# Moving part of a third row tile and one operand sum in a fused attention and MoE kernel

## The chip, the cores and the metric

The kernel runs on one core of one Trainium2 chip. The time is the device time of one execution in microseconds (us); the figure before is the median of three runs. One further execution was recorded by the hardware profiler, and every start and duration below is from that one.

The engines are named as in the profile: PE is the matmul engine (PEld its weight loads), DVE the vector engine, ACT the scalar engine, POOL the GpSimd engine, SP the queue that issues most DMAs. Each runs its own instructions in the order written. PSUM, where matmuls leave their results, has eight banks.

## What is computed

For 8 batches, 12 heads, 448 tokens and a head dimension of 64, attention with normalised q and k, followed by two matrix products with a leaky relu between them:

```python
q_n, k_n = rmsnorm(q, g_q), rmsnorm(k, g_k)
scores = (1 / sqrt(64)) * q_n @ k_n.T
attn = exp(scores - max(scores)); attn = attn / (sum(attn) + 1e-9)
x = (attn @ v) as rows of tokens            # 3584 x 768
h = x @ w_in                                # w_in: 768 x 2048
g = maximum(0.01 * h, h)
out = g @ w_out                             # w_out: 2048 x 768
```

Both w_in and w_out are the same for all tokens. Inputs and output are 32-bit floats; operands of the matmuls are rounded to 16 bits.

## The kernel before

**Attention.** The work is cut into 24 units `u`, each four heads of one batch, so three units make a batch. For a unit the kernel loads q and k (`load`), squares them (`prep_sq`), sums the squares (`prep_ssq`, line 186), forms the inverse root on ACT with a logarithm and an exponential (`prep_rinv`, 191 and 192), multiplies (`prep_norm`, 198) and transposes the result. Units up to 5 are transposed by PE matmuls (`prep_tr`, 210) that are copied out of PSUM by DVE, later ones by a DMA. The scores are computed for seven key tiles of 64 (`score`, 228), in four steps `d` = 0 to 3: key tile 0 in step 0 and the other six in steps 1 to 3. The exponential (`ex`, 243) subtracts a shift taken from key tile 0 alone. The shift's chain runs over three engines: DVE takes the maximum (257) and spreads it on a diagonal (259), PE multiplies this with a matrix of ones (276, or 282 in unit 3), and DVE reduces the product (277, 283) and forms the bias (287). The products with v (403), the sums of the exponentials (302, 313 or 340) and their inverse (387 to 394, or 361 and 366) give the attention output, which `xmul` (412) or line 381 multiplies into the tile `xt`, the operand of the first MoE product.

**First MoE product.** Per batch there are 16 row tiles `ft` of 128 of the hidden dimension, and each is a sum over six tiles `kt` of 128 of the model dimension, two from each unit of the batch. `moe1` (425) does one row tile in one bank, with six matmuls, then `prelu` (419) on ACT. For batch 0, row tiles 0 and 1 are done earlier, by `moe1_part` (433), in pieces between steps of units 2 and 3, into a pair of banks called `first`. Pieces 0 and 1 come from unit 0, 2 and 3 from unit 1, 4 and 5 from unit 2.

**Second MoE product.** Most token tiles are done in pairs by `seven`: seven block products in place of eight, with sums of operands. s1 to s4 (505 to 514) are DVE operations over blocks of `gt` and give the four blocks of the tile `sa`; the products `i0` to `i6` are PE items of eight matmuls each (535). i3 reads block 0 of sa, i4 block 2, i5 block 3 and i1 block 1. A call may be given the next pair of tiles, `nxt`, and then also issues s1 to s4 for that pair. The product banks are called ma, mb, mc and md; DVE adds (542) collect them into output tiles that SP stores.

**The order of the work** is written out by hand. `push` puts the items of one batch on a list, `queue`. `PLAN` has, for each unit from 3 on, a string of four digits, and the digit of step d is the number of items that `fill` takes from the list there. An item leaves its trailing DVE, ACT and store operations on a second list, `pend` (`later`), and the next item calls `flush`, which issues them before its own matmuls. At the end of step 3, flush can keep s1 to s4 back. In step 0 the order is: the scores of key tile 0, the maximum and the diagonal, flush, the products with v, the sums, the matmul with ones, the bias, the first exponential, then the items of the step.

In batches 1, 3 and 5 the first of two calls of `seven` has `nxt` and is not `mixed`. There i3 and i4 are the two items of step 3 of units 8, 14 and 20, and i5 and i6 the two items of step 0 of units 9, 15 and 21. In batch 7 the call is mixed, which means that parts of i0, i1 and i3 are issued in another order.

**The banks** are handed out from the list `free`. Up to unit 4, `aux` gives the longest free one of banks 0 to 3 and `slot` a pair out of banks 4 to 7; from unit 5 on all eight are shared. `drop` puts banks back at the end of the list.

Of the kernel before, what the change touches and what calls it, by code (L numbers as in the profile page):

```python
# [13 lines left out]
ts = bass.ts  # L14
# [4 lines left out]
def kernel(  # L19
# [11 lines left out]
    nc = tc.nc  # L31

    B, H, S, D = q.shape
    QH = 4
    NS = 7
    P = 128
# [3 lines left out]
    KT = DM // P  # L40
# [20 lines left out]
    def mine(i):  # L61
        return shared or i < 4
# [7 lines left out]
    def aux(bank=None):  # L70
        can = [i for i in free if mine(i) and bank in (None, i)]
        if shared:
            can = [i for i in can[:-1] if i ^ 1 not in free] or can
        free.remove(can[0])
        return single[can[0]]
# [12 lines left out]
    def drop(tile_):  # L88
        for i in range(8):
            if tile_ is single[i]:  # L90
                assert i not in free
                free.append(i)
                return
        x = [i for i in range(4) if tile_ is double[i]][0]
        assert 2 * x not in free and 2 * x + 1 not in free
        free.extend((2 * x, 2 * x + 1))
# [21 lines left out]
    win16 = cst.tile([P, NQ, 2, DF], FP16)  # L118
    wout16 = cst.tile([P, FT, DM], FP16)
    gt = cst.tile([P, FT, 8 * 64], FP16)  # L120
# [44 lines left out]
    def buf(u, name):  # L165
        if name not in st[u]:
            shape, dtype, bufs = SHAPES[name]
            st[u][name] = prep_p.tile(shape, dtype, tag=name[:2] if bufs == 3 and name != "qkT" else name, bufs=bufs, name=name)
        return st[u][name]
# [14 lines left out]
    def prep_ssq(u, c=ALL, tis=BOTH):  # L184
        for ti in tis:
            nc.vector.tensor_reduce(buf(u, "ssq")[:, ti, :, c[0]:c[1]], buf(u, f"sq{ti}")[:, :, c[0]:c[1]],  # L186
                                    axis=AXL.X, op=ALU.add)

    def prep_rinv(u, tis=BOTH):
        x = slice(tis[0], tis[-1] + 1)  # L190
        nc.scalar.activation(buf(u, "uu")[:, x], buf(u, "ssq")[:, x], AF.Ln, bias=eps_t, scale=1.0 / D)
        nc.scalar.activation(buf(u, "rinv")[:, x], buf(u, "uu")[:, x], AF.Exp, bias=0.0, scale=-0.5)  # L192
# [102 lines left out]
    xts = {}  # L295
# [119 lines left out]
    def prelu(b, dst, src):  # L415
        if b % 2 == 0:
            src = src.rearrange("p (t x) -> p t x", t=NS)[:, ::-1]
            dst = dst.rearrange("p (t x) -> p t x", t=NS)
        nc.scalar.activation(dst, src, AF.Prelu, bias=0.0, scale=1.0, alpha=0.01)  # L419
# [10 lines left out]
    def moe1_part(b, banks, k0, k1):  # L430
        for ft in range(2):
            for kt in range(k0, k1):
                nc.tensor.matmul(banks[:, ft, 0:S], win16[:, kt // 2, kt % 2, ts(ft, P)], xts[b][:, kt // 2, kt % 2],  # L433
                                 start=(kt == 0), stop=(kt == KT - 1))
# [4 lines left out]
    def store(pair, t, tile_, c, last):  # L439
        for y in range(2):  # L440
            n = 2 * t + (1 - y if t < 3 else y)
            b, grp = 2 * pair + n // NS, n % NS
            dst = out[b * S:(b + 1) * S, :].rearrange("(p t) m -> p t m", t=NS)
            eng = nc.scalar if last and y else nc.sync
            eng.dma_start(dst[:, grp, c], tile_[64 * y:64 * y + 64, c])
# [5 lines left out]
    def flush(keep=0):  # L451
        kept = [p for p in pend if keep and (p[0] in (s1, s2, s3, s4) or hasattr(p[0], "waits") or keep == 5 and hasattr(p[0], "copies"))]
        now = [p for p in pend if p not in kept]
        pend[:] = kept
        for fn, args in now:
            fn(*args)

    def out_tile():
        return opool.tile([P, DM], FP32, tag="ost", name="ost")
# [32 lines left out]
    def wblock(i, j):  # L492
        return wout16[:, HF * i:HF * i + HF, HC * j:HC * j + HC]
# [7 lines left out]
    def gblock(t, j):  # L501
        return gt[:, HF * j:HF * j + HF, ds(col(t), P)]
# [24 lines left out]
    def later(fn, *args):  # L527
        pend.append((fn, args))

    def seven(pair, tt, nxt=None, last=False, mixed=False):  # L530
        g = {}

        def mm(bank, a, b, first, fs=range(HF)):
            for f in fs:
                nc.tensor.matmul(bank[:, 0:HC], a[:, f], b[:, f], start=(first and f == 0), stop=(f == HF - 1), skip_group_check=not first)  # L535

        def bank(name):
            g[name] = aux()
            return g[name]

        def add(dst, src, name):
            nc.vector.tensor_tensor(dst, g[name][:, 0:HC], src, op=ALU.add)  # L542

        def put(i, c):
            store(pair, tt[i], g["o"][i], c, last)

        def i0():
            flush()
            g["o"] = (out_tile(), out_tile())
            ma = bank("ma")  # L550
            if mixed:
                mm(ma, gblock(tt[0], 0), wblock(0, 0), True, range(6))
                mm(bank("mb"), sa[:, 1], tw[:, 1], True, range(4))
            mm(ma, gblock(tt[0], 0), wblock(0, 0), True, range(6 if mixed else 0, HF))
            if mixed:
                mm(bank("mc"), sa[:, 0], tw[:, 0], True, range(4))
            later(lambda: nc.vector.tensor_copy(g["o"][1][:, L], g["ma"][:, 0:HC]))

        def i1():
            flush()  # L560
            mm(g["mb"] if mixed else bank("mb"), sa[:, 1], tw[:, 1], True, range(4 if mixed else 0, HF))
            later(lambda: add(g["o"][1][:, L], g["o"][1][:, L], "mb"))
            later(lambda: drop(g["mb"]))

        i1.merged = True

        def i2():
            flush()
            mm(g["ma"], gblock(tt[0], 1), wblock(1, 0), False)
            later(lambda: nc.scalar.copy(g["o"][0][:, L], g["ma"][:, 0:HC]))  # L570
            later(lambda: drop(g["ma"]))
            if last:
                later(put, 0, L)

        def i3():
            flush()
            mm(g["mc"] if mixed else bank("mc"), sa[:, 0], tw[:, 0], True, range(4 if mixed else 0, HF))
            later(lambda: add(g["o"][1][:, R], g["o"][1][:, L], "mc"))
            if nxt:
                later(s1, nxt)  # L580

        def i4():
            flush()
            mm(bank("md"), sa[:, 2], tw[:, 2], True)
            later(lambda: add(g["o"][1][:, R], g["o"][1][:, R], "md"))
            if last:
                later(put, 1, R)

        i4.merges = True

        def i5():
            flush()
            mm(g["mc"], sa[:, 3], wblock(1, 1), False)
            if nxt:
                later(s2, nxt)
            later(lambda: add(g["o"][0][:, R], g["o"][1][:, L], "mc"))
            later(lambda: drop(g["mc"]))
            later(put, 0, R if last else LR)
            if nxt:
                later(s3, nxt)  # L600
                later(s4, nxt)

        def i6():
            flush()
            mm(g["md"], gblock(tt[1], 1), tw[:, 3], False)
            def end():
                add(g["o"][1][:, L], g["o"][1][:, L], "md")
                drop(g["md"])
                put(1, L if last else LR)

            end.waits = True
            later(end)

        return [i0, i1, i2, i3, i4, i5, i6]

    HK = KT // 2
# [124 lines left out]
    queue = []  # L741
# [8 lines left out]
    def push(b):  # L750
# [32 lines left out]
        else:  # L783
# [8 lines left out]
            items += [(1.31, fn) for fn in std]  # L792
        queue.extend(items)

    PLAN = ("2122", "1222", "2112", "2122", "3232", "3322", "2322",
            "3222", "3232", "2222", "3323", "3232", "2322", "3222",
            "3232", "2222", "3323", "3232", "2322", "4356", "5232")
    STEPS = ((0,), (1, 2), (3, 4), (5, 6))
# [11 lines left out]
    def fill(u, d, jobs):  # L810
        for n in range(int(PLAN[u - 3][d])):
            fn = queue.pop(0)[1]
            fn()
            if jobs and not (d == 2 and (u == 12 and hasattr(fn, "merges") or u in (14, 20) and hasattr(fn, "merged"))):
                jobs.pop(0)()
        flush(keep=u if d == 3 and u < NU - 1 else 0)
        for job in jobs:
            job()
# [30 lines left out]
    with tc.manual_schedule():  # L849
# [56 lines left out]
        shift_mm(0)  # L906
        drop(st[0]["pb"])
        prep_ssq(1)

        def trn(u, ti, copy):  # L910
            prep_tr(u, ti, ((ALL, copy),))
# [32 lines left out]
        k1 = []  # L944
# [104 lines left out]
        ex(3)  # L1049
        prep_rinv(4)  # L1050
        moe1_part(0, first, KT - 2, KT - 1)
        moe1_part(0, first, KT - 1, KT)
        for ft in range(2):
            prelu(0, gt[:, ft, 0:S], first[:, ft, 0:S])
        drop(first)
        del queue[0:2]

        for u in range(3, NU):
            for d in range(4):
# [141 lines left out]
```

## Time and profile before

| | |
|---|---|
| median of three runs | 409.06 us (408.88 to 409.59) |
| profiled execution | 408.8 us |
| its span, first to last instruction | 406.9 us |
| PE busy | 396.7 us (97%), 3876 matmuls |
| DVE busy | 311.3 us (76%) |
| ACT busy | 303.9 us (75%) |
| POOL busy | 70.6 us (17%) |
| granted clock of PE | 1.000 |
| L505, s1 | 15 times, seven over 128x1024 and eight over 128x512 |

A row of the timeline gives start, duration, engine, line, instruction, output and inputs, shapes and the number of instructions merged into it. In square brackets stands how long the engine had been idle before it, and what released it. A matmul's duration reaches to the modelled end of its pipeline, so successive matmuls overlap in these rows, and the pitch from one start to the next is what they cost PE.

### The profile page before, as it was taken

Reading aid. Unit: us, or ns where it says so; the run is one execution under the profiler, and the core shown is the slowest. Engines: PE = TensorE matmul, PEld = TensorE weight load, DVE = VectorE, ACT = ScalarE, POOL = GpSimd, SP = SyncE. Lnnn points to the kernel's source line nnn. Section 1 sums busy time; section 2 is a strip of 40 time slices with the busy share of each in tenths; the row PEclk is TensorE's granted clock in tenths of the full one; section 3 lists DMA queues with packets and bytes.
Section 4 is the critical chain, followed back from the end, with each engine's and each line's share of the span. In section 5 each row is a group of like instructions: output and inputs, shape, how many; then the busy total and the mean of one; then the engine's idle time right before and its main releaser. Section 6 shows DMA issues by size and latency. Waiting matters only on the chain.

```text
span 406.9 us, 9527 instructions
## 1 busy us (share of the span) xinstructions
PE 396.7 (97%) x3876; PEld 225.0 (55%) x3876; DVE 311.3 (76%) x482; ACT 303.9 (75%) x474; POOL 70.6 (17%) x88
## 2 busy tenths in 40 slices
PE   8999999999999999999999999999999999999996
PEld 7665454555455544555455544555455557559963
DVE  5888999988879665886679756787679889567672
ACT  5998877788977699778978689868987667743600
POOL 1787432200120200120011200020002200000000
PEclk9999999999999999999999999999999999999999
DMA  6999999999455887478563795777732470022023
GB/s 197 276 235 251 240 235 246 236 223 213 96 156 110 239 216 117 135 198 192 137 159 66 226 218 116 187 178 170 177 72 49 122 169 0 20 68 79 0 57 99
DMA packets 72527, 62.87 MB, mean 154 GB/s; under 512 B 36389, under 2 KB 67621, under 8 KB 72485
## 3 DMA queue, kind: packets, MB, share of 16 engines
q1 hardware_dynamic: 61888, 50.08, 46.3%
q0 software_dynamic: 10272, 11.80, 18.8%
q8 instruction: 30, 0.49, 0.5%
q10 hardware_dynamic: 324, 0.39, 0.3%
q14 instruction: 13, 0.10, 0.1%
HBM read 45.61 MB, written 11.01 MB: 139 GB/s over the span
## 4 chain that ended last, share of the span: by engine, by line
PE 87%; DVE 2%; issue 0%; DVEq 0%
PE banks L425 29%; PE banks L535 25%; PE banks L228 9%; PE banks L471 8%; PE banks L669 6%; PE banks L403 6%; PE banks L340 3%; PE banks L276 1%; DVE banks L257 1%; DVE ost L542 1%; PE banks L210 0%; PE banks L433 0%; DVE xt L412 0%; DVE dg L259 0%; PE banks L313 0%
## 5 line engine op out<-in xcount | busy, mean ns | idle before, releaser
L243 ACT ACTIVATE et<-banks,eb 128x896 f16<-128x896 f32 x168 | 160.6, 1008 | 22.8 <-PE banks L228 22.1
L425 PE MATMUL banks<-xt,win 128*128 128x448 f16 x612 | 122.2, 353 | 0.0
L425 PEld LDWEIGHTS <-win 128*128 128x128 f16 x612 | 57.6, 98 | 56.2 <-issue 6.9
L419 ACT ACTIVATE gt<-banks 128x448 f16<-128x448 f32 x104 | 55.2, 551 | 9.1 <-PE banks L425 7.6
L186 DVE TENSOR_REDUCE ssq<-sq 128x14 f32<-128x896 f32 (+2 forms) x49 | 50.3, 1058 | 0.8 <-ACT sq L175 0.8
L228 PE MATMUL banks<-qkT 64*64 64x448 f16 x672 | 49.0, 361 | 1.6 <-DVE qkT L824 0.8
L535 PEld LDWEIGHTS <-sa 128*128 128x128 f16 x352 | 33.4, 98 | 26.1 <-issue 5.1
L535 PE MATMUL banks<-tw,sa 128*128 128x384 f16 x264 | 46.9, 326 | 0.0
L542 DVE TENSOR_TENSOR ost<-banks,ost 128x384 f32<-128x384 f32 x55 | 30.4, 553 | 13.2 <-PE banks L535 12.3
L257 DVE TENSOR_REDUCE banks<-banks 128x1 f32<-128x896 f32 x24 | 26.3, 1098 | 15.1 <-PE banks L228 11.1
L403 PE MATMUL banks<-et,vt 64*64 64x448 f16 x672 | 36.9, 349 | 0.0
L535 PEld LDWEIGHTS <-gt 128*128 128x128 f16 x264 | 25.5, 98 | 18.2 <-issue 1.7
L198 DVE TENSOR_TENSOR n<-rq,rinv 128x896 f16<-128x896 f32 (+2 forms) x25 | 33.1, 1328 | 1.9 <-ACT rinv L192 1.9
L471 PE MATMUL banks<-wout,gt 128*128 128x384 f16 x192 | 33.7, 326 | 0.0
L228 PEld LDWEIGHTS <-qkT 64*64 64x64 f16 x672 | 16.6, 105 | 29.1 <-issue 21.8
L535 PE MATMUL banks<-wout,gt 128*128 128x384 f16 x176 | 32.4, 326 | 0.0
L293 POOL COPY gate_t<-qkT 128x1 f16<-128x1 f16 x16 | 4.0, 251 | 152.3 <-DMA qkT<-n 152.3
L198 DVE TENSOR_TENSOR n<-rk,rinv 128x896 f16<-128x896 f32 (+2 forms) x26 | 26.1, 1012 | 0.0
L403 PEld LDWEIGHTS <-vt 64*64 64x64 f16 x672 | 20.0, 107 | 10.0
L471 PEld LDWEIGHTS <-gt 128*128 128x128 f16 x192 | 18.0, 98 | 13.7 <-issue 2.9
L325 DVE TENSOR_TENSOR ea<-et 128x896 f16<-128x896 f16 x14 | 10.0, 714 | 18.2 <-ACT et L243 18.2
L381 POOL TENSOR_TENSOR xt<-x,rz 128x896 f16<-128x896 f32 x8 | 16.6, 2077 | 32.3 <-DMA rz<-zs 26.0
(109 smaller groups left out, 492.4 us busy)
## 6 DMA issues: line engine op xcount, KB each, us to landing
rq<-in_q_dram SPq DMA_DIRECT2D x24, 448.0 KB, 5.2
rk<-in_k_dram SPq DMA_DIRECT2D x24, 448.0 KB, 6.0
out_dram<-ost SPq DMA_DIRECT2D x52, 192.0 KB, 3.0
rz<-zs SPq DMA_DIRECT2D x80, 112.0 KB, 3.6
vt<-in_v_dram POOLq DMA_DIRECT2D x24, 224.0 KB, 5.3
win<-in_moe_w_in_dram POOLq DMA_DIRECT2D x8, 384.0 KB, 14.7
wout<-in_moe_w_out_dram POOLq DMA_DIRECT2D x2, 1536.0 KB, 28.4
out_dram<-ost SPq DMA_DIRECT2D x4, 96.0 KB, 2.1
```

What stands on the lines that cost most here:

```text
L186: nc.vector.tensor_reduce(buf(u, "ssq")[:, ti, :, c[0]:c[1]], buf(u, f"sq{ti}")[:, :, c[0]:c[1]], axis=AXL.X, op=ALU.add)
L198: nc.vector.tensor_tensor(buf(u, "n16")[:, ti, c[0]:c[1]].rearrange("p s a d -> p a s d"), src[:, :, c[0]:c[1]], buf(u, "rinv")[:, ti, :, ...
L228: nc.tensor.matmul(banks[a][64 * r:64 * r + 64, 0:S].rearrange("p (t x) -> p t x", t=NS), kT(u, r, a, t), qT(u, r, a), start=True, stop=True)
L243: nc.scalar.activation(s["et"][:, t], sT[:, :, 0:S], AF.Exp, bias=s["eb"], scale=1.0)
L257: nc.vector.tensor_reduce(s["spare"][:, 511:512], sT[:, :, 0:S], axis=AXL.XY, op=ALU.max)
L403: nc.tensor.matmul(s["pv"][r][64 * a:64 * a + 64, 0:S], vts[u % NV][64 * r:64 * r + 64, a, t], s["et"][64 * r:64 * r + 64, t, a], start=(t ...
L419: nc.scalar.activation(dst, src, AF.Prelu, bias=0.0, scale=1.0, alpha=0.01)
L425: nc.tensor.matmul(hps[:, 0:S], win16[:, kt // 2, kt % 2, ts(ft, P)], xt[:, kt // 2, kt % 2], start=(kt == 0), stop=(kt == KT - 1))
L471: nc.tensor.matmul(op2[:, 0:HC], gt[:, ft, ds(col(t), P)], wout16[:, ft, ds(HC * half, HC)], start=(i == 0), stop=(i == FT - 1))
L535: nc.tensor.matmul(bank[:, 0:HC], a[:, f], b[:, f], start=(first and f == 0), stop=(f == HF - 1), skip_group_check=not first)
L542: nc.vector.tensor_tensor(dst, g[name][:, 0:HC], src, op=ALU.add)
L669: nc.tensor.matmul(bank[:, HX * i:HX * i + HX].rearrange("p (t x) -> p t x", t=NS), w, x[:, kt], start=start, stop=(kt == HK - 1), skip_gr ...
```

## The change

There are two edits.

The first one is at the place where batch 0's row tiles 0 and 1 are finished. A new function, `moe1_third`, issues `moe1`'s matmuls of row tile 2 for a range of kt. Its first four are put between kt 4 and kt 5 of the first two row tiles, its last two behind kt 5, and its prelu behind the two others. Row tile 2 is taken off the list, and the first digit of `PLAN` goes from 2 to 1, so that all later steps get the same items as before.

The second edit concerns `seven` where it is not mixed: s1 of the next pair is left on `pend` by i5, just ahead of s2, where i3 left it before.

```diff
@@ seven, i3
-            if nxt:
+            if nxt and mixed:
                 later(s1, nxt)
@@ seven, i5
             flush()
             mm(g["mc"], sa[:, 3], wblock(1, 1), False)
             if nxt:
+                if not mixed:
+                    later(s1, nxt)
                 later(s2, nxt)
             later(lambda: add(g["o"][0][:, R], g["o"][1][:, L], "mc"))
             later(lambda: drop(g["mc"]))
@@ PLAN
-    PLAN = ("2122", "1222", "2112", "2122", "3232", "3322", "2322",
+    PLAN = ("1122", "1222", "2112", "2122", "3232", "3322", "2322",
@@ new function
+        def moe1_third(bank, k0, k1):
+            for kt in range(k0, k1):
+                nc.tensor.matmul(bank[:, 0:S], win16[:, kt // 2, kt % 2, ts(2, P)], xts[0][:, kt // 2, kt % 2],
+                                 start=(kt == 0), stop=(kt == KT - 1))
@@ ahead of the loop over units
         moe1_part(0, first, KT - 2, KT - 1)
+        third = aux()
+        moe1_third(third, 0, KT - 2)
         moe1_part(0, first, KT - 1, KT)
+        moe1_third(third, KT - 2, KT)
         for ft in range(2):
             prelu(0, gt[:, ft, 0:S], first[:, ft, 0:S])
+        prelu(0, gt[:, 2, 0:S], third[:, 0:S])
         drop(first)
-        del queue[0:2]
+        drop(third)
+        del queue[0:3]
```

## The prediction

> **What bounds the kernel now.** I read the page first (busy shares, clock row, the chain that ended last), then the waits of the matmul engine (PE) alone, stretch by stretch, then the chain and the timeline around each wait. The page gives PE 97% busy, its clock full in all 40 slices, and the chain that ended last runs 87% through PE. So time is won only where PE stands idle. Its waits over the whole span, as "engine line waited for: us in total, times, longest us":
>
> ```profile
> PE banks L276 <- DVE dg L259: 1.2, 3, 0.4
> ...
> PE banks L433 <- DVE xt L412: 0.5, 1, 0.5
> ```
>
> The same view cut into stretches shows none from 48 us to the end but the three of L276, at 125.67, 219.03 and 312.56. PE is unbroken between them, and what one of them gives up moves the end, unless something else then makes PE wait. The other row is the single stall at 42.48. The change touches exactly these two rows.
>
> The first of the three, in order of time (start us, us, engine, line, instruction):
>
> ```profile
> 121.68 1.08 DVE L198 TENSOR_TENSOR n<-rk,rinv 128x896 f16<-128x896 f32 x1
> 122.68 0.54 DVE L542 TENSOR_TENSOR ost<-banks,ost 128x384 f32<-128x384 f32 x1
> ...
> 123.14 0.68 DVE L505 TENSOR_TENSOR sa<-gt 128x1024 f16<-128x1024 f16 x1
> ...
> 123.74 0.55 DVE L542 TENSOR_TENSOR ost<-banks,ost 128x384 f32<-128x384 f32 x1
> 124.21 1.08 DVE L257 TENSOR_REDUCE banks<-banks 128x1 f32<-128x896 f32 x1
> ...
> 125.18 0.10 PEld L276 LDWEIGHTS <-onesp 128*128 128x128 f16 x1 [0.18 <-issue]
> 125.33 0.29 DVE L259 TENSOR_TENSOR dg<-ident,banks 128x128 f16<-128x128 f16 x1
> 125.67 0.22 PE L276 MATMUL banks<-dg,onesp 128*128 128x128 f16 x1 [0.42 <-DVE dg L259]
> ```
>
> VectorE (DVE) is the late one: it comes from a 2.92 us normalisation at 118.83, then does the add of i3, s1 (L505), the add of i4, and only then the shift's maximum (L257) and diagonal (L259), while PE has its weights for L276 at 125.18. The scores that L257 reads ended near 123.33, long before its start.
>
> The stall at 42.48:
>
> ```profile
> 41.19 0.58 ACT L394 ACTIVATE rz<-rz 128x448 f32<-128x448 f32 x1
> ...
> 41.80 0.62 DVE L412 TENSOR_TENSOR xt<-banks,rz 128x448 f16<-128x448 f32 x1
> ...
> 42.34 1.08 DVE L186 TENSOR_REDUCE ssq<-sq 128x14 f32<-128x896 f32 x1
> 42.48 0.54 PE L433 MATMUL banks<-xt,win 128*128 128x448 f16 x2 [0.50 <-DVE xt L412]
> ...
> 45.07 1.09 DVE L198 TENSOR_TENSOR n<-rk,rinv 128x896 f16<-128x896 f32 x1
> 45.22 0.14 PEld L228 LDWEIGHTS <-qkT 64*64 64x64 f16 x8 [0.37 <-issue]
> ...
> 45.72 0.89 PEld L210 LDWEIGHTS <-n 128*128 128x128 f16 x14 [0.36 <-issue]
> ```
>
> What to see: behind the stall, PE's transposes of unit 4's k need the n that DVE ends at 45.07 + 1.09 = 46.16. That chain runs over L394, L412, L186, Ln and Exp at 43.46 and 43.81, and the norms at 44.06 and 45.07. No PE work of after 41 us is in it.
>
> **Part 1, the third row tile.** Nothing is added or removed in all: six matmuls, one prelu and one bank move from step (3,0) to before it. The 12 matmuls of L425 that follow the stall take 2.27 us, 0.19 each. After the change four of them fill 41.98 to 42.74; the last key tile of the first two, ready at 42.44, goes at 42.74, 0.26 later than now; two for the third follow to 43.5, and row tile 3 to 44.6. PE then reaches the scores of (3,1) at 45.22 - 0.50 = 44.72 and the transposes at 45.22. The first seven have their n since 45.15. The second seven are held by 46.16. They are held there today already: cut finely, the weight loads of the first seven are over by 46.12, none runs until 46.22, and there they resume, 0.06 after DVE's end. So the 0.50 is not saved but moves to 45.7, and PE's work from 46.22 on stands where it stood: **0.00**. Cover for the 0.26 and for the earlier prelu: ScalarE (ACT) starts its four prelus at 43.94 behind rinv, whatever PE does, and the third tile is complete near 43.5; without that cover 0.26 would be paid. The bank: the third takes bank 1, last read by an L392 that started at 40.63 and took 0.53; row tile 3 then takes bank 2 and the free list at (3,1) is the old one, so no later bank changes. The weights are those that row tile 2 reads today. No DMA moves with it. Bounds: -0.50, if the transposes were not held, and +0.26, if the cover failed; I take 0 because the hold is a row of the trace.
>
> **Part 2, s1 behind the chain.** In the three non-late odd batches, s1 leaves the flush of i4, at (8,3), (14,3), (20,3), for the flush of i6, behind the shift's chain of the next unit. Three instructions of 0.68 us move; none is added, no DMA, no wait.
>
> Before the chain: the add of i4 now starts at 123.74. It reads what the add of i3 writes, which ends at 122.68 + 0.54 = 123.22; dependent DVE instructions follow after some 0.03 (s1 at 116.34 for 0.42, s2 at 116.79). PE's i4 ended near 123.0. So it starts at 123.25, 0.49 earlier, and L257, L259 with it: dg ends at 125.13 and L276 could start at 125.18. PE's own side: its weights are loaded at 125.18, and an unhindered L276 starts 0.01 after its load (at 80.62 and 80.63), so 125.19. Both sides allow 125.67 - 125.19 = 0.48. The second place gives 219.03 - 218.56 = 0.47 (DVE: 217.10 - 216.62 = 0.48), the third 312.56 - 312.09 = 0.47 (DVE 0.49). **Sum 1.42.** The lower bound is the printed waits, 0.42 + 0.41 + 0.41 = 1.24; the upper is DVE's 0.60 from s1's start to the next start, three times 1.80, which PE's own readiness cuts off. I take 1.42, because it goes by starts.
>
> A rule speaks against it. The Trainium skill, VectorE: DVE Perf Modes, section "The DRAIN you can't avoid", says that after each DVE operation a flush of about its duration less 266 ns has to pass before the next one starts. By that an add of 0.54 would hold the next for another 0.27, the gain would be near 0.24 a place and 0.72 in all. Here 122.68 to 123.14 is 0.46 from start to start, less than the first one's duration, so I go by the rows.
>
> Behind the chain: s1 now stands between eb (L287) and s2. Today s2 starts at 126.40 and the adds follow. After, L277 is released either by L276 (125.5) or by ACT's copy at L355, which ends at 124.77 + 0.91 = 125.68 and is named as the releaser of L277 five times elsewhere. Take the later: L277 at 125.70, eb at 126.03, s1 126.10, s2 126.70, the add to mc 127.30, s3 127.77, s4 128.37, the add to md 128.97 to 129.52 (pitches 0.60 and 0.47, as now). So DVE runs at most 0.1 behind today while PE runs 0.48 ahead. Who waits for that: i0 of the next seven takes mc's bank at 129.18 - 0.48 = 128.70, free from 127.86, slack 0.84; i1 takes md's bank one item of 1.30 later, at 130.0, free from 129.52, slack 0.48; sa block 1 is needed at 130.0 and done at 127.4. The store (SP queue) waits for the mc add, 0.1 later at most. That the writes of s1 and s2 don't wait for i5's matmuls is seen today: s2 starts at 126.40 while they read sa until 127.19. DVE catches up in its 1.58 us of idling before 134.58. So I cost this side at nothing; with the 0.48 used up, every further tenth costs 0.1 a place.
>
> **Sum.** 0.00 - 1.42: the span goes from 406.9 to 405.5 and the profiled execution from 408.8 to 407.4, 1.9 us lying outside the span. That execution is 0.26 under the median of 409.06; the same step from the median gives 409.06 - 1.42 = 407.64, forecast **407.65**.
>
> **Rivals.**
> - *The transposes let go as well.* Part 1 keeps its 0.50: 409.06 - 1.42 - 0.50 = 407.15. For it: PE is idle at 42.0 by the profile. Against: the loads that resume at 46.22, 0.06 behind n. Chance 0.05.
> - *A half gain.* The add of i4, or L257, starts later than reckoned, or L276 finds another wait, so that a place gives half, 0.24: 409.06 - 0.72 = 408.35. For it: two sides of the sum meet within 0.01 us, so any delay on DVE's counts. Against: the start-to-start rows. 0.11.
> - *The stall is replaced.* PE wins 0.48 at L276 and waits as long for something else before the unit ends: 409.06. For it: DVE is 76% busy and carries s1 in any case. Against: the slack of 0.48 and no PE wait from 126 to 216 today. 0.08.
> - *Slower: md's bank.* The add to md in i6's tail, now queued behind s1 and s2, ends after i1 wants the bank. PE then waits, and it decides for a loss once that add is late by more than 0.48 of slack plus the 0.48 won, 0.96. One more pair of the reductions of L186 ahead of it on DVE (2.07 us for two, as at 47.46) would cost 2.07 - 0.96 = 1.11 a place: 409.06 + 3.33 = 412.4. For it: 0.48 is a thin slack, and a normalisation beside POOL's product took 2.92 instead of 1.08 at 118.83. Against: in the order written out, the only jobs between i5 and i6 are ACT's exponentials and loads. 0.06.
>
> The forecast keeps 0.70. **Range** 407.1 to 408.6: below, the first rival; above, the half gain with the median's own scatter (the three runs lie within 0.7). Apart from the rivals the forecast's own range is 407.3 to 408.0. What a measurement can tell from no change is 0.2%, 0.8 us. Faster by more: the forecast, the first rival and about a third of the half gain, 0.79; within it: the rest of the half gain and the replaced stall, 0.15; slower 0.06.
>
> **What would show it.** In the profile after: the row "L276 waits for dg" is gone or at 0.1 in all, L505 (128x1024) stands behind L287 at all three places, and L257 starts 0.5 after the scores' first matmul instead of 1.3. For part 1: no wait at L433, but a PE wait for n at L210 of about 0.5 near 46.2, and PE's row tile 4 starts where it starts now, near 46.6. Wrong would be: a PE wait at L535 or L425 between 126 and 132, a wait at L210 under 0.3, or L276 still waiting 0.2 or more.

## The result and the profile after

The changed kernel takes **407.66 us** (median of 7 runs, 407.21 to 408.14) against 409.06 (7 runs, 408.36 to 409.59): a ratio of 0.9965, 95% interval 0.9953 to 0.9976. That is 1.4 us, and between 1.0 and 1.9 by the interval. The profiled execution took 407.55, its span 405.7. Faster, by an amount that can be told from no change, and close to the forecast of 407.65. How close is partly luck, as the terms below show.

The waits of PE over the whole span, after (engine, line, waited for: us in total, times, longest us):

```profile
PE banks L840 <- DVE onesp L107: 1.2, 1, 1.2
PE banks L210 <- DVE n L198: 1.0, 2, 0.6
PE banks L228 <- DVE qkT L826: 0.8, 2, 0.4
PE banks L228 <- ACT et L243: 0.7, 4, 0.2
PE banks L885 <- DVE n L198: 0.4, 1, 0.4
PE banks L302 <- DVE qkT L826: 0.2, 1, 0.2
```

The rows of L276 and L433 are gone. L210 had one wait of 0.6 before, at 33.70 us; it now has a second one of 0.4. From 48 us to the end PE waits for nothing that the profile names.

The first of the three places, in order of time:

```profile
122.81 1.21 DVE L542 TENSOR_TENSOR ost<-banks,ost 128x384 f32<-128x384 f32 x2
...
123.94 1.09 DVE L257 TENSOR_REDUCE banks<-banks 128x1 f32<-128x896 f32 x1
...
125.06 0.29 DVE L259 TENSOR_TENSOR dg<-ident,banks 128x128 f16<-128x128 f16 x1
...
125.32 0.10 PEld L276 LDWEIGHTS <-onesp 128*128 128x128 f16 x1 [0.18 <-issue]
125.40 0.22 PE L276 MATMUL banks<-dg,onesp 128*128 128x128 f16 x1
...
125.72 0.30 DVE L277 TENSOR_REDUCE banks<-banks 128x1 f32<-128x128 f32 x1 [0.38 <-PE banks L276]
...
126.13 0.68 DVE L505 TENSOR_TENSOR sa<-gt 128x1024 f16<-128x1024 f16 x1
...
126.85 0.69 DVE L508 TENSOR_TENSOR sa<-sa,gt 128x1024 f16<-128x1024 f16 x1
...
129.13 0.55 DVE L542 TENSOR_TENSOR ost<-banks,ost 128x384 f32<-128x384 f32 x1
...
130.15 1.46 PE L535 MATMUL banks<-tw,sa 128*128 128x384 f16 x8
```

The two adds (x2) now run back to back and L257 follows at once; s1 (L505) stands behind the bias. PE's multiplication with ones starts 0.08 behind its weight load, where it was 0.49 before. The last two rows are md's release and i1, which takes that bank: 129.13 + 0.55 = 129.68 against 130.15.

Around the transposes, the place of the first edit (L914 is the third row tile):

```profile
41.97 0.92 PE L914 MATMUL banks<-xt,win 128*128 128x448 f16 x4
...
42.72 0.54 PE L433 MATMUL banks<-xt,win 128*128 128x448 f16 x2
...
45.22 1.08 DVE L198 TENSOR_TENSOR n<-rk,rinv 128x896 f16<-128x896 f32 x1
...
45.41 0.56 PE L210 MATMUL banks<-ident,n 128*128 128x128 f16 x7
...
46.36 0.56 PE L210 MATMUL banks<-ident,n 128*128 128x128 f16 x7 [0.39 <-DVE n L198]
...
46.76 1.30 PE L425 MATMUL banks<-xt,win 128*128 128x448 f16 x6
```

The stall at 42.5 is filled, and 4 us later the transposes of k stand still until DVE's n, 45.22 + 1.08 = 46.30. Row tile 4 starts at 46.76. Before, it started at 46.62, in a profile in which everything from 39.8 on lies 0.15 earlier.

To read such small shifts, all profiles are set at the start of `moe1_part`'s second group of matmuls (40.63 before). The table gives, in us and good to 0.01, how much earlier (-) or later (+) L276 starts than in the first profile of before, and how the last matmul's end moves. The columns are named by the start before. 55.84 lies behind the first edit; 125.67, 219.03 and 312.56 are the three places of the second.

| kernel | 55.84 | 125.67 | 219.03 | 235.07 | 312.56 | end |
|---|---|---|---|---|---|---|
| changed kernel | -0.01 | -0.42 | -0.84 | -1.01 | -1.42 | -1.43 |
| e1, second edit alone | -0.01 | -0.42 | -0.84 | -1.01 | -1.42 | -1.43 |
| e2, first edit alone | -0.01 | -0.02 | -0.04 | -0.21 | -0.22 | -0.22 |
| e3, row tile 4 between | -0.38 | -0.80 | -1.22 | -1.39 | -1.80 | -1.52 |
| e4, s1 twice ahead | -0.01 | +0.72 | +1.45 | +1.59 | +2.32 | +2.31 |
| e5, add behind | -0.01 | -0.51 | -0.98 | -1.14 | -1.63 | -1.63 |
| e6, s3 three times | -0.01 | -0.42 | +0.61 | +1.62 | +1.20 | +2.38 |
| e7, both moves | -0.37 | -0.88 | -1.35 | -1.51 | -2.00 | -2.00 |
| e8, e3 without the first edit | +0.05 | -0.39 | -0.79 | -0.97 | -1.37 | -1.07 |
| e9, before once more | -0.01 | -0.01 | -0.01 | -0.19 | -0.18 | -0.19 |
| e10, e3 with small settings | -0.37 | -0.79 | -1.20 | -1.37 | -1.76 | -1.77 |
| e11, e7 once more | -0.37 | -0.87 | -1.33 | -1.49 | -1.97 | -1.96 |
| e12, e5 once more | -0.01 | -0.49 | -0.96 | -1.12 | -1.60 | -1.59 |

### The profile page after: what moved, and what is told of

Its sections match the earlier page's. It is cut to its first block, busy times and chain, and to the rows that moved or that the text cites. A ratio compares the mean times of both kernels' runs of the same rounds, so it can differ in the third digit from the quotient of the medians.

```text
span 405.7 us, 9527 instructions
## 1 busy us (share of the span) xinstructions
PE 396.8 (98%) x3876; PEld 225.2 (56%) x3876; DVE 310.3 (76%) x482; ACT 303.6 (75%) x474; POOL 71.0 (17%) x88
## 4 chain that ended last, share of the span: by engine, by line
PE 88%; DVE 1%; issue 0%; ACT 0%
PE banks L425 29%; PE banks L535 25%; PE banks L228 9%; PE banks L471 8%; PE banks L403 7%; PE banks L671 6%; PE banks L340 3%; PE banks L276 1%; DVE n L198 1%; PE banks L210 0%; DVE ssq L186 0%; PE banks L433 0%; PE banks L313 0%; DVE xt L412 0%; DVE ost L542 0%
## 5 line engine op out<-in xcount | busy, mean ns | idle before, releaser
L535 PEld LDWEIGHTS <-sa 128*128 128x128 f16 x352 | 33.4, 98 | 24.9 <-issue 3.9
L535 PE MATMUL banks<-tw,sa 128*128 128x384 f16 x264 | 46.9, 326 | 0.0
L257 DVE TENSOR_REDUCE banks<-banks 128x1 f32<-128x896 f32 x24 | 26.3, 1098 | 15.4 <-PE banks L228 12.2
L535 PEld LDWEIGHTS <-gt 128*128 128x128 f16 x264 | 25.5, 98 | 18.0 <-issue 1.4
L198 DVE TENSOR_TENSOR n<-rq,rinv 128x896 f16<-128x896 f32 (+2 forms) x25 | 32.0, 1281 | 2.4 <-ACT rinv L192 2.4
L535 PE MATMUL banks<-wout,gt 128*128 128x384 f16 x176 | 32.4, 326 | 0.0
L570 ACT COPY ost<-banks 128x384 f32<-128x384 f32 x11 | 5.3, 478 | 22.7 <-PE banks L535 22.7
```

The source lines that it names most:

```text
L198: nc.vector.tensor_tensor(buf(u, "n16")[:, ti, c[0]:c[1]].rearrange("p s a d -> p a s d"), src[:, :, c[0]:c[1]], buf(u, "rinv")[:, ti, :, ...
L257: nc.vector.tensor_reduce(s["spare"][:, 511:512], sT[:, :, 0:S], axis=AXL.XY, op=ALU.max)
```

## The experiments

### The two edits apart (e1, e2)

e1 is the kernel before with only this:

```diff
-            if nxt:
+            if nxt and mixed:
                 later(s1, nxt)
...
             if nxt:
+                if not mixed:
+                    later(s1, nxt)
                 later(s2, nxt)
```

> Only the second edit: s1 behind the shift's chain, row tile 2 where it was before. Theory (the first edit is worth nothing, because the stall it fills comes back at the transposes of unit 4's k): the time of the changed kernel, 407.7, within 0.2%, and L276 at the three places 0.4 earlier each, relative to the place before. Rival (the first edit is worth its 0.5 of filled stall): 408.2, and PE's row tile 4 some 0.5 later than in the changed kernel.

e2 is the rest of the change: `moe1_third`, its calls, the shorter list and PLAN "1122".

> Only the first edit: part of the third row tile ahead of the last key tile, s1 where it was. Theory: no change, 409.1; no wait at L433, a wait of 0.4 at the transposes (L210) in its place, and L276 still waiting 0.4 at the three places. Rival (the stall is saved): 408.6, and every later start 0.5 earlier.

Measured: e1 407.76 (10 runs), ratio 0.9960 (0.9947 to 0.9973); e2 408.81 (11 runs), ratio 0.9990 (0.9980 to 1.0000), both beside 409.15. PE's waits from 39 us on, in e1:

```profile
PE banks L433 <- DVE xt L412: 0.5, 1, 0.5
```

and in e2:

```profile
PE banks L276 <- DVE dg L259: 1.2, 3, 0.4
PE banks L210 <- DVE n L198: 0.4, 1, 0.4
```

e1 keeps the stall at L433 and still stands, from 55.84 to the end, within 0.01 of the changed kernel. e2 exchanges one row for another and has won 0.01 at 55.84. So by the traces the second edit is the whole gain, and the first is worth nothing by itself, as forecast: its stall comes back at the transposes. Of the 0.22 that e2 shows at the end, 0.17 come from the stretch between 219 and 235, which is taken up at e9.

### Is PE held by n and by nothing else? (e3, e8)

e3 puts other work where PE now stands still. On top of the changed kernel:

```diff
-    PLAN = ("1122",
+    PLAN = ("1022",
...
                     for ti in range(2):
                         prep_tr(u + 1, ti, VV)
+                        if u == 3 and ti == 0:
+                            queue.pop(0)[1]()
```

> The changed kernel with one more move: in step (3,1) the item of that step, row tile 4 of the first product, goes between the transposes of unit 4's q and those of its k. Theory (PE is held there by DVE's n for k and by nothing else): the six matmuls, 1.14, cover the hold of 0.39; PE waits no more at L210 near 46.4 and all later starts are 0.35 to 0.4 earlier: 407.3. Rival (the hold was never worth time, since ACT's exponentials bound that stage): the wait is gone but the scores of (3,2) wait for ACT in its place, 407.7.

e8 does the same without the first edit (PLAN "2022", row tile 2 in its old place).

> The second edit alone (row tile 2 where it was before), with row tile 4 between the transposes of unit 4's q and k. Theory (without the first edit the transposes are hardly held, 0.06, so that there is little to cover, while the stall of 0.50 at 42.5 stays): 407.7, and 0.35 to 0.4 more than the same move on top of the changed kernel. Rival (the move alone brings the gain, the first edit has no part in it): the time of that one, 407.3.

Measured in e3, in order of time:

```profile
45.44 0.56 PE L210 MATMUL banks<-ident,n 128*128 128x128 f16 x7
...
45.84 1.30 PE L425 MATMUL banks<-xt,win 128*128 128x448 f16 x6
...
46.98 0.56 PE L210 MATMUL banks<-ident,n 128*128 128x128 f16 x7
```

Row tile 4 covers the hold, no wait is printed there, and the table has 0.38 at 55.84, which stays until 312.56. e8 has +0.05 there, so the same move costs a little where the transposes are not held. The move puts the copy of k (L826) behind row tile 4 and DVE's later work with it, so that L276 waits for the diagonal: in e8 its weights are there from 56.57, the diagonal ends at 56.40 + 0.29 = 56.69, and it starts at 56.74. By the traces the first edit is therefore worth 0.43 once something covers the hold, and nothing without it. ACT, the rival, did not take the place of the wait.

In the medians the gain of e3 did not show: 407.87 (8 runs), ratio 0.9966 (0.9952 to 0.9980), and e8 407.95 (11 runs), 0.9977 (0.9968 to 0.9985). Part of this is in the last column: both lose some 0.3 at the last unit's shift. In e3:

```profile
343.15 0.34 PE banks L228 x4
343.49 0.12 issue
343.61 0.06 DVE u L684
343.67 0.48 issue
344.15 1.10 DVE banks L257
```

(the chain that ended last: start, length, what it runs through). A DVE add, L684, starts at 343.61, though DVE had been idle for 0.26 and PE's matmuls for it were over at 343.15. It starts 0.90 after the add before it, where the changed kernel has 0.54. e10 looks at this.

### How PE's wait hangs on DVE's queue (e4)

On the kernel before, i3 leaves s1 twice:

```diff
             if nxt:
                 later(s1, nxt)
+                if not mixed:
+                    later(s1, nxt)
```

> The kernel before, with s1 issued twice in a row where it stood before the change (the second writes the same values again), in the three batches concerned: 0.60 more DVE work ahead of the shift's chain at three places. Theory (the length of DVE's queue ahead of the chain sets PE's wait at L276, one for one): L276 waits 1.0 in place of 0.4 at each, 409.06 + 1.8 = 410.9. Rival (the wait at L276 is set by something else, and s1 gave way to another delay): 409.1 to 409.5.

Measured: 411.06 (9 runs), ratio 1.0044 (1.0031 to 1.0056), 1.9 above the 409.15 beside it. PE's waits from 48 us on:

```profile
PE banks L276 <- DVE dg L259: 3.4, 3, 1.1
PE banks L535 <- DVE ost L542: 0.2, 1, 0.2
```

The wait grows from 0.4 to 1.1 a place, and by the table the places cost 0.73 each (0.72 + 0.01, 1.45 - 0.72, and 2.32 - 1.59, nothing having moved between 235.07 and the third). Forecast was 0.60. The mechanism holds one for one, and the difference is in DVE: the two s1, which write the same block, together take 1.40 us, so the second starts 0.72 after the first and not 0.60. The wait at L535 is taken up at e9.

### What is left at L276 (e5, e12)

The add of i4 is kept over step 3 as well, in the calls with `nxt` that are not mixed, and so is issued behind L259:

```diff
-            later(lambda: add(g["o"][1][:, R], g["o"][1][:, R], "md"))
+            def late_add():
+                add(g["o"][1][:, R], g["o"][1][:, R], "md")
+
+            late_add.waits = bool(nxt and not mixed)
+            if not late_add.waits:
+                del late_add.waits
+            later(late_add)
```

> The changed kernel with the add of i4 kept back too, at the three places, so that DVE issues it behind the shift's maximum and diagonal (L257, L259) and ahead of the reduction L277. Theory (what is left of the stall, L276 0.08 behind its weights in place of 0.01, is the second of two dependent adds starting 0.12 behind the first): L276 0.01 behind its weights, 0.07 a place and 0.2 in all, 407.4. Rival (the 0.08 is the diagonal's own lag, or DVE delays the bias now and with it ACT): 407.7 or more.

> The kernel with the add of i4 behind the diagonal alone, once more: 407.2 to 407.6, and 0.37 slower than the one with both moves if its row tile 4 keeps what it won to the end; the same time if it does not.

Measured in e5:

```profile
122.64 0.55 DVE L542 TENSOR_TENSOR ost<-banks,ost 128x384 f32<-128x384 f32 x1
123.43 1.10 DVE L257 TENSOR_REDUCE banks<-banks 128x1 f32<-128x896 f32 x1 [0.24 <-PE banks L228]
124.56 0.29 DVE L259 TENSOR_TENSOR dg<-ident,banks 128x128 f16<-128x128 f16 x1
124.77 0.55 DVE L542 TENSOR_TENSOR ost<-banks,ost 128x384 f32<-128x384 f32 x1
125.16 0.10 PEld L276 LDWEIGHTS <-onesp 128*128 128x128 f16 x1 [0.18 <-issue]
125.16 0.23 PE L276 MATMUL banks<-dg,onesp 128*128 128x128 f16 x1
```

Now L257 waits for the scores and not for DVE, the diagonal is done before PE wants it, and L276 starts with its weight load. A place gives 0.50, 0.48 and 0.48 in e5 and 0.49, 0.48 and 0.48 in e12, which is PE's whole readiness as the prediction had it. Times: 407.18 (5 runs) beside 408.96, ratio 0.9959 (0.9947 to 0.9970), and 407.45 (5 runs) beside 409.21, 0.9960 (0.9946 to 0.9973). Against the changed kernel's 0.9965 the intervals overlap; that this is 0.2 faster rests on the traces.

### The slack behind the chain (e6)

On the changed kernel, i5 leaves s3 three times in a row:

```diff
                 later(s3, nxt)
+                if not mixed:
+                    later(s3, nxt)
+                    later(s3, nxt)
                 later(s4, nxt)
```

> The changed kernel with s3 issued three times in a row (the same values) at the three places, which puts 1.2 more DVE work between the bias and the add to md. Theory (PE's i1 takes md's bank and has 0.47 of slack there): PE waits 1.2 - 0.47 = 0.7 at i1 a place, 407.7 + 2.2 = 409.9. Rival (more slack than reckoned, the add is not what i1 waits for): 407.7.

Measured: 410.91 (4 runs) beside 408.96, ratio 1.0046 (1.0031 to 1.0061). In its trace:

```profile
127.84 2.14 DVE L511 TENSOR_TENSOR sa<-gt 128x1024 f16<-128x1024 f16 x3
...
130.50 0.55 DVE L542 TENSOR_TENSOR ost<-banks,ost 128x384 f32<-128x384 f32 x1
...
131.10 1.46 PE L535 MATMUL banks<-tw,sa 128*128 128x384 f16 x8 [0.87 <-DVE ost L542]
...
131.96 0.55 DVE L557 COPY ost<-banks 128x384 f32<-128x384 f32 x1
...
132.56 1.46 PE L535 MATMUL banks<-wout,gt 128*128 128x384 f16 x8
```

PE's i1 waits for the add to md, the rival that was named, and i1 starts 2.34 after i0 (128.76) where the changed kernel has 1.31: 1.03 lost. Forecast was 0.7. The three s3 follow each other at 0.72 and 0.73 and not 0.60, so that 1.46 was added and not 1.2; less the slack of 0.47 that is 0.99. The slack is confirmed, and with it that the second edit stops half a microsecond short of a new stall. A place costs more than that. The product behind i1 starts 1.46 after it (131.10 to 132.56) where the changed kernel has 1.30 (130.15 to 131.45): by the trace's semaphores it waits for DVE's copy L557, which follows the late add and ends at 131.96 + 0.55 = 132.51. So 1.03 + 0.16 = 1.19 a place, 3.6 of the 3.8 that separate the two ends. The rest, 0.27, is lost at the L276 of 187.10, which waits for DVE's diagonal.

### The odd 0.17 (e9) and the odd 0.30 (e10)

Between 219.03 and 235.07 all later profiles are 0.16 to 0.18 shorter than the first one of before, except those of e4 and e6, which have waits of their own there. e9 is that kernel, unchanged.

> The kernel before, unchanged, profiled once more. In the first profile PE lost 0.16 between two products of eight matmuls at 231 us without a named wait, and no profile of another kernel shows it there. If that belongs to this program, it returns: 0.16 more than in the changed kernel between the L276 of 219 and that of 235 us. If it was one execution's, the stretch has the length that it has in the changed kernel, 15.87.

Measured: 408.54 (one run). The stretch in the first profile of before:

```profile
227.71 2.08 POOL L381 TENSOR_TENSOR xt<-x,rz 128x896 f16<-128x896 f32 x1 [6.17 <-ACT rinv L192]
228.41 2.32 DVE L198 TENSOR_TENSOR n<-rq,rinv 128x896 f16<-128x896 f32 x1
...
229.77 1.47 PE L535 MATMUL banks<-wout,sa 128*128 128x384 f16 x8
230.66 0.54 DVE L542 TENSOR_TENSOR ost<-banks,ost 128x384 f32<-128x384 f32 x1
...
231.25 1.46 PE L535 MATMUL banks<-tw,gt 128*128 128x384 f16 x8
```

and in e9:

```profile
228.32 1.59 DVE L198 TENSOR_TENSOR n<-rq,rinv 128x896 f16<-128x896 f32 x1
...
229.67 1.47 PE L535 MATMUL banks<-wout,sa 128*128 128x384 f16 x8
229.83 0.55 DVE L542 TENSOR_TENSOR ost<-banks,ost 128x384 f32<-128x384 f32 x1
...
230.98 1.46 PE L535 MATMUL banks<-tw,gt 128*128 128x384 f16 x8
```

The second product starts 1.48 after the first in one and 1.31 in the other: the gap does not return. It was one execution's, and no part of the change's gain. It is a wait after all. By the trace's semaphores the second product waits for DVE's add, which ends at 231.20, 0.05 ahead of its start; no view prints the wait, because the idle time up to it, taken from the modelled end of the matmul before, is only 0.01. In e4 the same wait is longer, and so it is printed (L535, 0.2). The add is late because the normalisation before it took 2.32 and not 1.59. It ran beside POOL's product L381 for 1.38 (228.41 to 229.79), in e9 for 0.65 (L381 from 226.89 to 228.97), and the next normalisation, without POOL, took 1.08. L381 in turn starts 0.17 after the last transfer of `rz` has landed (227.54, in e9 226.72; the row names an ACT operation that ended at the same time). The transfer took 5.12 from its issue, in e9 4.40, and why is not shown.

Set against e9, the changed kernel's end moves by 1.43 - 0.19 = 1.24, which is the three places (0.41, 0.41, 0.40) and nothing else of size.

e10 is e3 with the constant `one32` set four times at the start:

```diff
+    nc.vector.memset(one32, 1.0)
+    nc.vector.memset(one32, 1.0)
+    nc.vector.memset(one32, 1.0)
     nc.vector.memset(one32, 1.0)
```

> The changed kernel with row tile 4 between the transposes, and three more settings of one small constant by DVE at the start. In the kernel without these, an add of DVE at 343.61 began 0.4 later than its inputs were ready and PE lost 0.30 of its 0.38 at the shift of the last unit. Theory (it hangs on where instructions lie in DVE's stream): the loss goes or moves, and the gain of 0.38 stays to the end of the span. Rival (the stage around the last unit's shift is bound by something that does not move with PE): the loss of 0.30 returns at the same L276.

Measured: 407.02 (one run). The loss is gone: of the 0.36 by which e10 is ahead of the changed kernel at 55.84, 0.34 is left at the end (-1.77 against -1.43). In e10 the add that was late in e3 comes without a gap (its line is now 687):

```profile
342.54 0.63 DVE L687 TENSOR_TENSOR banks<-banks,v 128x448 f32<-128x448 f32 x1
343.08 0.62 DVE L687 TENSOR_TENSOR u<-banks,u 128x448 f32<-128x448 f32 x1
```

The stage is not bound by something that stays put, so the rival falls. DVE's own operations come in the same order in e3 and e8 as in the changed kernel and e1, which do not have the late add. What differs is the number of entries in DVE's queue ahead of it, waits counted as the trace records them: 575 in e3 and e8, and 571, 572, 574 or 578 in the twelve other profiles, which all start that add 0.54 after the one before. That fits the theory of the place in the stream. It is two profiles against twelve, and what makes the add late is not shown.

### Both moves (e7, e11)

e3's and e5's moves together, on the changed kernel.

> The changed kernel with both moves, row tile 4 between the transposes and the add of i4 behind the diagonal. Theory: the gains add, 0.39 + 0.2: 407.1. Rival: only one of them counts, 407.3 or 407.5.

> The kernel with both moves once more, beside the one with the add alone, on one chip: 0.37 faster than that one by the traces so far, 406.9 to 407.4.

Measured: 407.38 (9 runs, 406.67 to 408.77), ratio 0.9961 (0.9949 to 0.9973), then 406.83 (5 runs), ratio 0.9948 (0.9935 to 0.9960), beside e12's 407.45. So e11 is 0.62 ahead of e12 in the medians and 0.37 in the table, where 0.37 was expected. In both traces the gains add, -2.0 and -1.96 at the end, and in e11 no wait of PE is named from 39 us to the end. Both are faster than the kernel before; that e7's version beats the changed kernel's 0.9965 is shown by the traces (0.53 to 0.57 at the end), while the intervals of the times overlap.

## Why the prediction was right

**Part 1, 0.00: right.** The hold by DVE's n was read from a row of the trace, and it decided: 0.01 at 55.84 with the edit and without it (e1, e2). PE's new wait at L210 is 0.39; about 0.5 was expected. The cover for the third tile's prelu held too: ACT's four prelus start at 44.08, which is 43.94 and the 0.15 by which the profile is shifted.

**Part 2, 1.42: the mechanism right, one term too large.** The places give 0.41, 0.41 and 0.40, together 1.22, where 0.48, 0.47 and 0.47 were forecast. The mis-sized step is "dependent DVE instructions follow after some 0.03". Taken singly, the adds of i3 and i4 start at 122.81 and 123.46, and the first ends at 123.36. So the second comes 0.10 behind that end, 0.07 later than reckoned, and the diagonal is as much later. DVE's side was said to meet PE's within 0.01, and so all of this counts. With that add out of the way (e5, e12) the forecast 0.48 appears. The lower bound, the printed waits with 1.24, was the better value.

The 0.03 was read from s2 behind s1. s2 holds its one wait, for s1, itself. The second add waits for two things, the first add and PE's product, and in the trace the wait for the first add is an entry of its own in DVE's queue, at 123.40. In all fourteen profiles the DVE operations that the one before them lets go start 0.03 after its end (the median) where they hold that wait themselves, and 0.10 where an entry stands between. The profile of before has such a pair of adds as well, and its row shows the 1.21:

```profile
180.08 1.21 DVE L542 TENSOR_TENSOR ost<-banks,ost 128x384 f32<-128x384 f32 x2
```

One of the signs did not fit the sum. L257 was to start 0.5 after the scores' first matmul instead of 1.3; by the sum's own 0.49 that is 124.21 - 122.95 - 0.49 = 0.77, and 0.85 was measured (123.94 - 123.09). And PE was said to be unbroken between the three places; the 0.17 at 231.25 (e9) shows that a printed list of waits does not say that.

**The sum, 407.65: right, and 0.2 of its closeness is chance.** By the traces the change is worth 1.24 (against e9); the medians say 1.40, with an interval of 1.0 to 1.9. The forecast of 1.42 lies inside, and so does 1.24, so the times alone cannot tell them apart.

**Behind the chain, nothing: right.** The adds were placed with pitches of 0.60 and 0.47 and a late L277. L277 came earlier (125.72, before the copy of L355 ended at 125.81, so that copy does not release it here), s1 to s2 took 0.72 and not 0.60, and the two deviations cancel: md's slack is 0.47 where 0.48 was reckoned, and e6 shows that it is real.

**The rule on the flush.** The Trainium skill, VectorE: DVE Perf Modes, "The DRAIN you can't avoid", would by the prediction's estimate have put the second add 0.27 behind the first one's end, with 0.24 a place. The same section adds that an operation that is not held starts earlier. The dependent pair measured 0.10, and 0.41 a place; independent neighbours overlap (0.46 from start to start before the change, for an add of 0.54). The measurement decides: some gap is there behind a dependent operation, less than the page's flush.

None of the rivals came. The half gain came closest: its reason, DVE's side later than reckoned, is what cost 0.07 a place.

## What to carry to other kernels

Before filling a stall, look for the next place where the same engine waits for the chain that made it wait: here the filler moved 0.5 us by 4 us and saved none of it, until other work was put in front of that second place. An operation that nobody needs yet, standing ahead of a chain on an in-order engine, costs the chain its whole length; put it behind, and count the slack of whatever then comes later, since here it was 0.47. When two engines are reckoned ready at the same moment, every hundredth of the one that is reckoned later counts, and here the printed wait was a better price than a difference of starts. A pitch is to be read from the same pair of operations, waits and all, where the profile has one.

## What was not expected of the hardware

A DVE instruction that waits for the one before it is dearer than one that does not, and how much dearer hangs on how it waits. Two s1 on the same block follow at 0.72, three s3 at 0.72 and 0.73, while operations of the same size that do not meet start at 0.60, before the one ahead has ended. For the adds out of PSUM, where the wait is an entry of its own, the pitch is 0.65 where both touch the same output and 0.46 to 0.47 otherwise.

A DVE normalisation is stretched by the time that it runs beside POOL's product: 2.32 with 1.38 beside it, 1.59 with 0.65, 1.08 alone. So the landing of a transfer moved PE by 0.17 in one execution and not in the next, over POOL, DVE and a wait too short to be printed.

A single instruction can also be late with no wait that the trace shows: some 0.35 on DVE, at the same add in two kernels, gone when three tiny instructions were put at the start. Each of these is as large as the effects studied here, so that a shift of a few tenths between two profiles is to be located before it is explained.
